# Reordering the write-out of the last two token groups: adds first, gates after both adds, a separate buffer for the last copy

## The chip, the cores and the metric

The kernel runs on one core of a Trainium2 chip. The metric is device time of one execution in microseconds (us).

Engines are called by the profile's short names: PE is TensorE, DVE is VectorE, ACT is ScalarE, POOL is GpSimd, SP is SyncE, which here issues the output transfers. A "q" behind a name (SPq) is that engine's sequencer.

## The reference, cut to what matters

```python
x = A_x                                  # (1, 2048, 1024) bf16
xn = _layernorm(x)
s = attention(xn, wqkv) @ wo             # 32 heads, window 8, dilation 2
g = silu(swiglu_mlp(xn, w1, w3, w2))     # hidden size 3584
return x + s * g                         # gate, then residual
```

Everything here takes place in the last stage: `@ wo` for the second half of the tokens, then `* g`, then `+ x`, then the transfer to memory.

## The kernel before

The large matrix products are done as seven half-size block products in place of eight (a Strassen-like scheme). For the output projection a group of 128-token tiles yields four blocks: 11, 12, 22 and 21 (first digit: half of the tokens, second: half of the columns). Blocks 11 and 21 come complete out of PE's accumulators and are copied by ACT. Blocks 12 and 22 need a saved PSUM tile added, by DVE. Each block is then multiplied by its gate and, in the second half of the tokens, gets its residual added (both DVE), and SP issues its transfer.

```python
def wo(b):
    ...
    for gp, ii in ((0, I), (1, I)) if b == 0 else ((0, I), (1, (0,)), (1, (1,))):
        ...                                    # the last group is cut in two for b == 1
        product(pa, gp, ii, a11, b11, True)    # tile "wa"
        product(pe, gp, ii, s1, t1, True)      # tile "we"
        flush()                                # the tail of the group before
        act_copy(pb, pa)                       # pb: tile "wb"
        act_copy(sp5, pe)                      # "wsp"
        ...
        product(pb, gp, ii, s2, t2, False)
        act_copy(su2, pb)                      # "wsu"
        steps = {
            "e12": lambda: (product(pe, gp, ii, s4, b22, False), finished(b, 0, 1, gp, ii, pe, su2)),
            "e22": lambda: (product(pb, gp, ii, s3, t3, False), finished(b, 1, 1, gp, ii, pb, sp5)),
            "e11": lambda: (product(pa, gp, ii, a12, b21, False), finished(b, 0, 0, gp, ii, pa)),
        }
        for k in ("e12", "e22", "e11") if n == 2 else ("e11", "e22", "e12"):
            steps[k]()

        def tail(gp=gp, ii=ii, pb=pb):         # block 21, in block 22's accumulator
            product(pb, gp, ii, a22, t4, False)
            finished(b, 1, 0, gp, ii, pb)
        ...

def finished(b, u, dh, gp, ii, ps, add=None):
    cut = slice(ii[0], ii[-1] + 1)
    g = g_tile(b, u, dh, gp)[:, cut]
    n = {(0, 0): 0, (1, 1): 2, (0, 1): 4, (1, 0): 0}[u, dh] + gp
    d = h_sb[:, 16 + 2 * n:18 + 2 * n, CH:][:, cut]
    rows_ = out_rows(out_flat, b, u, dh, gp)[:, cut]
    with hp():
        if add is None:
            nc.scalar.copy(out=d, in_=ps)                 # L956: blocks 11, 21
        else:
            nc.vector.tensor_add(d, ps, add)              # L958: blocks 12, 22
        anchor["v"] = nc.vector.tensor_mul(g, d, g)       # L959: gate
        if b == 0 or gp == 0:
            nc.gpsimd.dma_start(out=rows_, in_=g, accum_op=ALU.add)
        else:
            nc.vector.tensor_add(g, g, xw[u, dh][:, cut])  # L963: residual
            nc.sync.dma_start(out=rows_, in_=g)            # L964: transfer
```

A tile framework puts these instructions in order and adds the waits. Group names end in the order of the loop: the last two groups are `wa1_10` and `wa1_11` and so on; the profile leaves the numbers out. L151 is the matmul helper.

## Time and profile before

| | before |
|---|---|
| median of 3 runs | 723.38 us (723.37 to 723.46) |
| profiled execution | 723.18 us, span 721.5 us |
| last product of the last group begins on PE | 714.50 us |
| last DVE instruction ends | 717.39 us |
| last output transfer issued | 717.50 us |
| first matmul of this stage's first product | 690.99 us |

"Span" is what the trace covers; the time is 1.70 us more than it. The prediction shows the page, the chain and the timeline of the last microseconds. One view it names but doesn't show is that of the line that issues the output transfers, here for the time from 712 us on. Its columns are engine, operation, count, duration in ns as min/median/max, first and last start; the last line is the time from issue to landing of these five transfers.

```profile
L964 SPq DMA_DIRECT2D out_dram<-h_sb x5: 332/332/382, 712.7 to 717.5; - x5
...
DMA to landing us min/median/max: 1.7/1.7/3.0
```

Read it as: SP is occupied for 0.33 us by each issue; the data is in memory 1.7 us after the issue as a rule.

### The profile page before, as it was taken

What the parts mean: (1) busy time and instruction counts of PE and PEld (TensorE: products, weight loads), DVE (VectorE), ACT (ScalarE), POOL (GpSimd) and SP (SyncE); (2) the same over time, 40 slices, a digit from 0 to 9 for tenths busy, and PEclk for the clock granted to TensorE, in tenths of its full rate; (3) what the DMA queues carried; (4) which work ended last, traced back from release to release, by engine and by line L of the source; (5) the groups of instructions that cost most, each with busy time, mean ns of one, the idle gap of its engine ahead of it and who ended that gap; (6) DMA issues with size and microseconds to landing.
All of it is one profiled execution on the core that took longest, in us unless ns stands there. A gap on an engine that the chain in (4) does not pass through costs nothing.

```text
span 721.5 us, 8817 instructions
## 1 busy us (share of the span) xinstructions
PE 713.2 (99%) x3367; PEld 346.3 (48%) x3367; DVE 625.5 (87%) x697; ACT 314.0 (44%) x329; POOL 95.7 (13%) x162
## 2 busy tenths in 40 slices
PE   8999999999999999999999999999999999999996
PEld 6655565654444444444444444444444444444442
DVE  7996879779879878978999999969859989999964
ACT  5744334356555556545555312034364573020233
POOL 1011100012300000233111000000435005000011
PEclk9999999999999999999999999999999999999999
DMA  9956256787754523568756547469799444563615
GB/s 336 275 140 169 91 177 234 237 267 233 241 186 142 187 78 114 167 212 258 247 175 211 189 132 262 132 208 388 159 297 319 141 137 152 167 204 127 211 23 108
DMA packets 119242, 139.52 MB, mean 193 GB/s; under 512 B 17696, under 2 KB 94496, under 8 KB 118560
## 3 DMA queue, kind: packets, MB, share of 16 engines
q1 hardware_dynamic: 104656, 97.01, 42.7%
q0 software_dynamic: 14544, 41.95, 18.2%
q8 instruction: 26, 0.43, 0.2%
q14 instruction: 16, 0.13, 0.1%
HBM read 96.21 MB, written 38.80 MB: 187 GB/s over the span
## 4 chain that ended last, share of the span: by engine, by line
PE 95%; ACT 2%; DVE 2%; DMA 0%; issue 0%; DVEq 0%; ACTq 0%
PE bm L151 20%; PE am L151 13%; PE em L151 13%; PE db L151 10%; PE bq L151 9%; PE de L151 7%; PE da L151 7%; PE eq L151 6%; PE aq L151 3%; PE wb L151 2%; PE af L151 2%; PE wa L151 2%; PE we L151 2%; DVE h_sb L236 1%; PE af L1030 1%; DMA wring<-in_A_x_dram 0%
## 5 line engine op out<-in xcount | busy, mean ns | idle before, releaser
L151 PEld LDWEIGHTS <-wring 128*128 128x128 f16 (+1 forms) x1792 | 183.4, 102 | 204.3 <-issue 1.6
L151 PEld LDWEIGHTS <-h_sb 128*128 128x128 f16 (+1 forms) x1056 | 109.6, 104 | 118.1 <-issue 0.4
L151 PE MATMUL bm<-xs,wring 128*128 128x512 f16 x504 | 117.4, 379 | 0.1
L151 PE MATMUL am<-xT,wring 128*128 128x512 bf16 x336 | 79.7, 379 | 0.1
L151 PE MATMUL db<-wring,h_sb 128*128 128x512 f16 x336 | 73.2, 379 | 0.0
L481 DVE TENSOR_TENSOR BC<-Ep,vT 128x2048 bf16<-128x2048 bf16 x56 | 66.7, 1221 | 0.1
L426 DVE TENSOR_TENSOR pt<-qt,kT 128x4096 bf16<-128x4096 bf16 x24 | 55.0, 2292 | 0.6
L664 DVE TENSOR_TENSOR um<-em,um 128x1024 f32<-128x1024 f32 x28 | 34.2, 1223 | 21.0 <-PE em L151 20.2
L666 ACT ACTIVATE g<-um 128x1024 bf16<-128x1024 f32 x28 | 29.6, 1057 | 48.6 <-DVE um L664 48.6
L151 PE MATMUL da<-wring,h_sb 128*128 128x512 bf16 x224 | 49.0, 379 | 0.0
L467 POOL DMA_DIRECT2D Ep<-pb x64 | 38.0, 601 | 51.1 <-DVE pb L463 45.7
L151 PE MATMUL bm<-h_sb,wring 128*128 128x512 f16 x168 | 39.7, 379 | 0.0
L151 PE MATMUL em<-xT,wring 128*128 128x512 bf16 x168 | 39.7, 379 | 0.0
L151 PE MATMUL em<-xs,wring 128*128 128x512 f16 x168 | 39.7, 379 | 0.0
L491 DVE TENSOR_TENSOR oT<-oT,BC 128x2048 bf16<-128x2048 bf16 x32 | 39.1, 1221 | 0.3
L161 ACT COPY bm<-am 128x1024 f32<-128x1024 f32 x28 | 27.9, 998 | 25.8 <-PE am L151 25.8
L161 ACT COPY pm<-em 128x1024 f32<-128x1024 f32 x28 | 28.4, 1014 | 20.1 <-PE em L151 20.1
L161 ACT COPY um<-bm 128x1024 f32<-128x1024 f32 x28 | 28.4, 1014 | 18.9 <-PE bm L151 18.9
L685 ACT CAST g<-bm 128x1024 bf16<-128x1024 f32 x28 | 28.3, 1010 | 17.4 <-PE bm L151 17.4
L679 DVE TENSOR_TENSOR h_sb<-bm,pm 128x1024 bf16<-128x1024 f32 x21 | 25.6, 1219 | 5.1 <-PE bm L151 5.0
L428 DVE TENSOR_TENSOR pt<-pt 128x2048 bf16<-128x2048 bf16 x24 | 29.4, 1223 | 0.4
L489 DVE TENSOR_TENSOR BC<-BC 128x2048 bf16<-128x2048 bf16 x24 | 29.3, 1222 | 0.4
(191 smaller groups left out, 999.5 us busy)
## 6 DMA issues: line engine op xcount, KB each, us to landing
wring<-in_B_w_dram SPq DMA_DIRECT2D x61, 512.0 KB, 4.3
wring<-t_dram SPq DMA_DIRECT2D x16, 512.0 KB, 4.2
t_dram<-wring POOLq DMA_DIRECT2D x14, 512.0 KB, 3.9
wring<-t_dram SPq DMA_DIRECT2D x16, 384.0 KB, 5.0
wring<-in_B_w_dram SPq DMA_DIRECT2D x12, 384.0 KB, 4.5
wring<-in_A_x_dram SPq DMA_DIRECT2D x16, 256.0 KB, 4.8
Ep<-pb POOLq DMA_DIRECT2D x64, 64.0 KB, 4.7
wring<-in_A_wo_dram SPq DMA_DIRECT2D x8, 512.0 KB, 5.9
```

The costliest lines, as they stand in the source:

```text
L151: anchor["pe"] = nc.tensor.matmul(ps, lhsT=lhs[k], rhs=rhs[k], start=(first and k == 0), stop=(k == n - 1), skip_group_check=not first,)
L161: nc.scalar.copy(out=out_, in_=in_)
L426: nc.vector.tensor_mul(p_t[:], q[:], kT[:, :, o:o + CH])
L428: nc.vector.tensor_add(p_t[:, 0:4, :], p_t[:, 0:4, :], p_t[:, 4:8, :])
L467: nc.gpsimd.dma_start(out=pr[c][r:P:NR, :, sq * P:(sq + 1) * P], in_=pb[sq * 32:(sq + 1) * 32, :, :])
L481: nc.vector.tensor_mul(dst, E[:, w, :].unsqueeze(1).to_broadcast([P, n, CH]), vT[:, js, o:o + CH])
L489: nc.vector.tensor_add(B, B, C)
L491: nc.vector.tensor_add(A, A, B if w0 else C)
L664: v = nc.vector.tensor_add(su2[:], pe[:], su2[:])
L666: nc.scalar.activation(out=hl["g"][:, :, CH:], in_=su2[:], func=ACTF.Silu)
L679: anchor["v"] = nc.vector.tensor_add(h[:, :, CH:], pb[:], sp5[:])
L685: nc.scalar.copy(out=hl["g"][:, :, 0:CH], in_=pb[:])
```

## The change

The intent: DVE is overfull in the last microseconds. Blocks that need a PSUM add, the long kind of DVE instruction, should come early, while DVE still has idle time. Gate and residual of a block are put off until both adds are done. As block 11's gate now comes late, the last copy (block 21) may not reuse block 11's buffer and gets another one.

```diff
-            for k in ("e12", "e22", "e11") if n == 2 else ("e11", "e22", "e12"):
-                steps[k]()
+            rest = [steps[k]()[1] for k in ("e12", "e22", "e11")]
+            with behind("v2") if n == 1 else nullcontext():
+                rest[0]()
+            rest[1]()
+            rest[2]()
 
             def tail(gp=gp, ii=ii, pb=pb):
                 product(pb, gp, ii, a22, t4, False)
-                finished(b, 1, 0, gp, ii, pb)
+                finished(b, 1, 0, gp, ii, pb)()
...
-        n = {(0, 0): 0, (1, 1): 2, (0, 1): 4, (1, 0): 0}[u, dh] + gp
+        n = {(0, 0): 0, (1, 1): 2, (0, 1): 4, (1, 0): 4}[u, dh] + gp
...
             else:
-                nc.vector.tensor_add(d, ps, add)
-            anchor["v"] = nc.vector.tensor_mul(g, d, g)
-            ...
+                anchor["v2"] = nc.vector.tensor_add(d, ps, add)
+
+        def gate():
+            with hp():
+                anchor["v"] = nc.vector.tensor_mul(g, d, g)
+                ...                      # residual and transfer, as before
+        return gate
```

`behind("v2")` keeps the first gate behind the latest add in the order of issue.

## The prediction

> **What bounds the kernel now.** I read four views, from the whole to the place of the change. First the page: span, busy time and the summary of the chain that ended last.
>
> ```profile
> span 721.5 us, 8817 instructions
> ...
> PE 713.2 (99%) x3367; PEld 346.3 (48%) x3367; DVE 625.5 (87%) x697; ACT 314.0 (44%) x329; POOL 95.7 (13%) x162
> ...
> PE 95%; ACT 2%; DVE 2%; DMA 0%; issue 0%; DVEq 0%; ACTq 0%
> ```
>
> TensorE sets the time nearly everywhere: 95% of the chain is matmuls. A change that leaves the number of matmuls alone can win only where the chain is not on PE. The 2% for VectorE and 2% for ScalarE are the start and the end. The last stage is the output projection, done as seven block products. So I asked for the chain of work from 690 us on:
>
> ```profile
> 710.18 1.73 PE wb L151 x8
> 711.90 0.88 PE wa L151 x4
> 712.78 0.02 issue
> 712.80 0.59 ACT h_sb L956
> 713.40 0.02 issue
> 713.42 0.42 DVE h_sb L959
> 713.85 0.60 DVE h_sb L958
> 714.45 0.33 DVE h_sb L963
> 714.78 0.60 DVE h_sb L958
> 715.38 0.67 DVE h_sb L959 x2
> 716.05 0.34 DVE h_sb L963
> 716.38 0.34 DVE h_sb L959
> 716.72 0.33 DVE h_sb L963
> 717.05 0.34 DVEq L1264
> ```
>
> PE leaves the chain at 712.78 us, with the first product of the last group's output (block 11, tile wa) with three more products to come on PE. From 713.42 us on, DVE is the chain without a gap: L958 adds a PSUM tile to its saved copy (blocks 22 and 12), L959 multiplies by the gate, L963 adds the residual. The timeline of the same stretch gives the true starts:
>
> ```profile
> 711.75 0.42 DVE L959 TENSOR_TENSOR h_sb<-h_sb 128x512 bf16<-128x512 bf16 x1 [1.10 <-ACT h_sb L956]
> 712.21 0.42 DVE L963 TENSOR_TENSOR h_sb<-h_sb,xw 128x512 bf16<-128x512 bf16 x1
> 712.63 1.02 PE L151 MATMUL wb<-h_sb,oT 128*128 128x512 f16 x4
> 713.49 1.03 PE L151 MATMUL we<-wring,h_sb 128*128 128x512 bf16 x4
> 713.76 0.68 DVE L958 TENSOR_TENSOR h_sb<-wb,wsp 128x512 bf16<-128x512 f32 x1
> 714.50 1.02 PE L151 MATMUL wb<-wring,oT 128*128 128x512 f16 x4
> 715.60 0.59 ACT L956 CAST h_sb<-wb 128x512 bf16<-128x512 f32 x1 [2.22 <-PE wb L151]
> 716.63 0.76 DVE L963 TENSOR_TENSOR h_sb<-h_sb,xw 128x512 bf16<-128x512 bf16 x2
> ```
>
> The reader is to see three things. DVE idles from 712.63 to 713.42 while products finish, and is then overfull. The last product (block 21, wb at 714.50) comes late: four matmuls have a cadence of 0.86 us, so after 713.49 it could have begun at 714.35; it accumulates into the bank that block 22's add reads until 713.76 + 0.68 = 714.44. And its ScalarE copy ends at 715.60 + 0.59 = 716.19, while the last DVE instruction starts at 716.97 (716.63 + 0.76 - 0.42) and ends at 717.39: the end waits for DVE's queue, not for the last product. After that the last output transfer is issued at 717.50 and the median transfer of this line lands 1.7 us after issue; the rest up to 721.5 us is closing down, which the change doesn't touch.
>
> **What the Trainium skill says.** "VectorE: DVE Perf Modes", the perf-mode tier table: an add of two tensors runs at two elements per cycle with bf16 in SBUF, at one with a PSUM operand or fp32. The trace agrees: 0.68 us for an add from PSUM, 0.42 us for a bf16 one, of the same 512 columns. So a block that needs an add costs DVE more than one that is copied by ScalarE, and these are the blocks that the change puts first. The same page, "The DRAIN you can't avoid", says that the next operation waits for the pipe and that a semaphore adds nothing. [...]independent starts are 0.60 us apart behind an add and 0.34 behind a bf16 operation. It differs on the second: a residual add right behind the multiply it reads starts 712.21 - 711.75 = 0.46 us after it, 0.12 more. The measurement decides, and this 0.12 matters below. "Perfetto Trace Analysis", section "Optimizing Tensor Performance", wants independent matmul groups to rotate through PSUM banks so that emptying one overlaps the next; blocks 22 and 21 share a bank by construction, and the 0.15 us delay at 714.50 shows it.
>
> **The change part by part.** It removes and adds no arithmetic: the same matmuls, 20 DVE instructions, casts and transfers in the last two groups. I compared the instruction order of the two builds; outside the write-out they are alike.
>
> *The new PE order.* In each of the last two groups the products go 11, 22, 12, 21 before and 12, 22, 11, 21 after. Each is four matmuls, so slots stay at 711.74, 712.63, 713.49 and 714.50 in the last group. Block 12 needs ScalarE's copy of wb, which ends at 712.58, before its product ends at about 712.77; no new wait. Block 22's slot does not move, so its add cannot begin much before 713.76.
>
> *The new DVE order.* Block 12's add starts at about 712.77 + 0.11 = 712.88 (0.11 is the distance from a PE end to an idle DVE's start at 698.06 to 698.17), in time that was idle. It frees DVE at 713.48. Then block 22's add at 713.76, and the build has: multiply 12, multiply 22, residual 12, multiply 11, residual 22, residual 11, multiply 21, residual 21. Starts: 714.36, 714.70, 715.04, 715.37, 715.71, 716.04, 716.38; the last directly depends on the one before, so 716.38 + 0.46 = 716.84. End 716.84 + 0.42 = 717.26.
>
> *The sum.* Behind block 22's add, before had a residual add, a PSUM add and six more bf16 operations; after has eight bf16 operations. One PSUM add (0.60) leaves the chain, and block 11's multiply (0.34) comes into it, because its product is now third: 0.26 us less. But the old order ended with two independent residual adds (0.34 apart), the new one ends with a dependent pair (0.46): 0.12-0.13 us given back. Net 717.39 - 717.26 = 0.13 us.
>
> *A possible extra.* Before, block 22's add started exactly one 0.34 cadence behind block 11's multiply (713.42), so DVE may have held it. Its product's end is modelled at 713.65; ready could be 713.69 to 713.76 if the distance is 0.04 to 0.11. Up to 0.07 us more, and the last product moves by the same amount. I take 0.03.
>
> *The buffer.* Block 21's cast formerly reused block 11's buffer; now that block's gate comes late, it reuses block 12's, read by a multiply that ends near 714.78, well before the cast at 715.60. Without this the cast would wait for multiply 11 (to 715.79), some 0.2 us; with it, nothing. The buffer preserves the gain rather than makes one.
>
> *Elsewhere.* In the full-size groups the gating order shifts a little; in the first group at 508.59 us multiply 12 gets ahead of add 22, whose end moves from 509.81 to about 510.4, and PE needs that bank at 510.77. Tight, but hidden. The second-to-last group is covered by PE work: zero.
>
> **The rivals.** (a) *The last product becomes the bound*: its cast ends at 716.19, multiply 21 could start by 716.21 and the end be 717.09. DVE still binds by 0.17, so this caps the gain at 0.30 us if something on DVE is cheaper than I count: 723.1. (b) *Nothing*: if multiply 11 or add 22 is released later than I assume, the dependent pair eats everything: 723.4. The closeness of 0.26 and 0.12 speaks for it. (c) *Issue of outputs becomes the bound*: SyncE takes 0.34 us for each transfer, and the four outputs now come at least 0.33 us apart, the last 0.8 behind the third; it speaks against it. A collision would cost at most 0.1: 723.4. (d) *A stall in the middle*: if the 510.77 margin fails, up to 0.3 us lost: 723.6.
>
> **Range and chances.** 723.38 - 0.13 - 0.03 = 723.22 us, taken as 723.2. The argument covers 723.0 to 723.6. The profiled execution took 723.18 where the timed ones took 723.37 to 723.46, so another session may sit some tenths off; I take 722.7 to 723.8. A change of 2% would be 14.5 us, more than twice the 6 us that lie behind PE's last product at 715.52: faster 0.005, within 2% 0.99, slower 0.005.
>
> **What would show it.** Right: in the last group add 12 starts near 712.9, add 22 at 713.70 to 713.76, eight bf16 operations follow without a gap but one of 0.12 before the last, which ends near 717.2; PE's four slots unmoved, and the last still about 0.1 late. Wrong: add 22 later than 713.8, a gap before multiply 11 or 21, the last transfer's issue more than 0.15 behind the last add, PE's chain longer at 510 us, or the whole span moved while this stretch gained.

## The result, and the profile after

| | before | changed |
|---|---|---|
| median | 723.38 us (6 runs, 723.27 to 723.46) | 721.87 us (6 runs, 721.79 to 722.62) |
| ratio | | 0.9981 (95%: 0.9969 to 0.9994), within 2% |
| profiled execution | 723.18 us, span 721.5 | 721.83 us, span 720.1 |

A ratio here is the mean time of one kernel's fast runs over the mean of the other's of the same rounds, so it isn't quite the ratio of the medians. The gain is small, but it is 1.51 us by the medians and 1.35 us by the profiled executions where 0.16 us had been predicted, and the time lies below the predicted range.

First the page of the changed kernel: the same counts of arithmetic, and three instructions more in all than the 8817 before.

```profile
span 720.1 us, 8820 instructions
...
PE 712.5 (99%) x3367; PEld 346.2 (48%) x3367; DVE 625.6 (87%) x697; ACT 314.1 (44%) x329; POOL 95.7 (13%) x162
```

Then the end of the chain, from the stretch before PE leaves it. The columns are start, length, engine, tile and line; L961 is now the PSUM add, L965 the gate, L969 the residual.

```profile
713.05 0.90 PE wb L151 x4
713.95 0.02 issue
713.98 0.69 DVE h_sb L961
714.67 0.67 DVE h_sb L965 x2
715.33 0.34 DVE h_sb L969
715.67 0.33 DVE h_sb L965
716.00 0.67 DVE h_sb L969 x2
716.67 0.34 DVE h_sb L965
717.02 0.02 issue
717.04 0.42 DVE h_sb L969
```

As predicted, the chain enters DVE with block 22's add, eight bf16 instructions follow it without a gap but one ahead of the last. The timeline of the changed kernel gives the starts:

```profile
712.02 1.03 PE L151 MATMUL we<-wring,h_sb 128*128 128x512 bf16 x4
...
712.91 1.02 PE L151 MATMUL wb<-h_sb,oT 128*128 128x512 f16 x4
713.16 0.69 DVE L961 TENSOR_TENSOR h_sb<-we,wsu 128x512 bf16<-128x512 f32 x1 [0.30 <-PE we L151]
713.77 1.03 PE L151 MATMUL wa<-wring,oT 128*128 128x512 bf16 x4
713.98 0.69 DVE L961 TENSOR_TENSOR h_sb<-wb,wsp 128x512 bf16<-128x512 f32 x1
...
714.72 1.02 PE L151 MATMUL wb<-wring,oT 128*128 128x512 f16 x4
...
716.59 0.42 DVE L965 TENSOR_TENSOR h_sb<-h_sb 128x512 bf16<-128x512 bf16 x1
717.04 0.42 DVE L969 TENSOR_TENSOR h_sb<-h_sb,xw 128x512 bf16<-128x512 bf16 x1
```

The last DVE instruction ends at 717.46, which is *later* on the clock than the 717.39 of before. The reason is the start of the kernel: the first matmul of the first large product comes at 8.84 us, before at 8.56, and the first matmul of the last stage at 691.27 instead of 690.99. The whole middle is 0.28 us late and otherwise unmoved. So times of different kernels are compared from here on **relative to the stage's start**, the first matmul of this output projection. On that scale the last add ends at 26.19 us in the changed kernel and at 26.40 us before, 0.21 us earlier.

But the span is 1.35 us shorter. Where is the rest? It is behind the last DVE instruction. The same view of the issuing line as above, now of the changed kernel:

```profile
L970 SPq DMA_DIRECT2D out_dram<-h_sb x5: 332/332/382, 712.9 to 717.5; - x5
...
DMA to landing us min/median/max: 1.7/1.7/1.7
```

The longest landing went from 3.0 to 1.7 us, and in the records of the trace before, the 3.0 us are the last transfer's. The view of what SP waits for, first before and then changed (total us, times, longest), says the same: L1264 and L1272 are the end of the program.

```profile
SPq L1264 <- DMA out_dram<-h_sb: 2.2, 2, 1.7
```

```profile
SPq L1272 <- DMA out_dram<-h_sb: 0.9, 2, 0.6
```

A transfer is carried out in 16 parts, each with its own completion in the trace. Before, 15 parts of the last transfer had landed at 719.25 and the 16th landed at 720.50, 1.25 us later. In the changed kernel the 16th landed 0.03 us after the 15th. What was in that part's way is in the list of DMA queues for the time from 716 us on, first before, then changed (packets, MB, share of the 16 engines):

```profile
DMA packets 452, 0.41 MB, mean 59 GB/s; under 512 B 58, under 2 KB 451, under 8 KB 451
...
q1 hardware_dynamic: 451, 0.40, 16.9%
q14 instruction: 1, 0.01, 0.3%
```

```profile
DMA packets 576, 0.52 MB, mean 75 GB/s; under 512 B 64, under 2 KB 576, under 8 KB 576
...
q1 hardware_dynamic: 576, 0.52, 21.4%
```

Before, one packet of kind "instruction" falls into this time: 8 KB, at 719.06 us, for 0.31 us. In the records, nothing of the last transfer moves after it except eight 1 KB packets, one part's worth (128 KB in 16 parts), which start from 719.36 to 719.99, five of them taking 84 to 152 ns where such a packet otherwise takes 46. In the changed kernel, the packet of this kind came at 714.76, before the last transfer was issued. It is an engine fetching its next stretch of program. The Trainium skill, "Runtime: NRT & Kernel Launch", section "Instruction fetch mechanics", says that each engine's instruction memory is a queue refilled in blocks through a DMA queue driven by the sequencer, at a cost "mostly hidden". The trace agrees in that the packets of kind "instruction" have queues of their own (q14 here); that one fetch is not hidden would be new.

So the difference behind the stage's start adds up as follows (relative times; each row is the difference of two of the trace's records, taken before rounding):

| | before | changed | gain |
|---|---|---|---|
| end of the last DVE add | 26.40 | 26.19 | 0.21 |
| from there to the last issue | 0.11 | 0.03 | 0.09 |
| from the issue to the last part's landing | 3.00 | 1.67 | 1.33 |
| last part's landing + closing down = span's end | 29.51 + 0.97 = 30.48 | 27.89 + 0.96 = 28.85 | 1.63 |
| stage's start | 690.99 | 691.27 | -0.28 |
| span | 721.48 | 720.13 | 1.35 |

Only the closing down, 0.97 and 0.96 us, is what the change doesn't touch.

### The profile page after: what moved, and what is told of

Same layout as the page of the kernel before. It is cut to its first block, busy times and chain, and to the rows that moved or that the text cites. A ratio compares the mean times of both kernels' runs of the same rounds, so it can differ in the third digit from the quotient of the medians.

```text
span 720.1 us, 8820 instructions
## 1 busy us (share of the span) xinstructions
PE 712.5 (99%) x3367; PEld 346.2 (48%) x3367; DVE 625.6 (87%) x697; ACT 314.1 (44%) x329; POOL 95.7 (13%) x162
## 4 chain that ended last, share of the span: by engine, by line
PE 93%; DVE 2%; ACT 1%; DMA 1%; issue 1%; SPq 0%; DVEq 0%; ACTq 0%
PE bm L151 20%; PE am L151 13%; PE em L151 13%; PE bq L151 9%; PE db L151 8%; PE da L151 7%; PE de L151 6%; PE eq L151 6%; PE aq L151 3%; PE wb L151 3%; PE af L151 2%; PE wa L151 1%; PE we L151 1%; PE af L1038 1%; DMA wring<-in_A_wqkv_dram 1%
```

## The experiments

**Theories.** T1: the landing depends on the instruction fetch, and the change moved the fetch out of the way because it altered the number of instructions of one engine. The build's order shows two more waits on DVE (block 12's add now waits for PE and ACT together, in each of the two groups), and the trace has 836 DVE records where before has 834, and 506 instead of 505 for ACT. T2 (rival): the landing depends on how the last transfers follow one another on SP; before, the last two were issued 0.42 us apart, now 0.71. T3 (rival): the 3.0 us is chance and any rebuild would lose it.

All results, each kernel with 5 runs beside the kernel before on the same chip (9 runs); the first two rows are the 6 runs each of the result above. Columns in the middle come from the trace's records of the profiled run, in us relative to the stage's start. "Against drain" is the last issue minus the end of DVE's drain (the DRAIN record behind DVE's last instruction; it ends 0.05 us after the last add). "16th part" is the landing of the last part minus that of the 15th.

| kernel | median us | ratio (95%) | last add ends | last issue | against drain | issue to landing | 16th part | fetch at | end of span |
|---|---|---|---|---|---|---|---|---|---|
| before | 723.38 | 1 | 26.40 | 26.51 | +0.06 | 3.00 | 1.25 | 28.06 | 30.48 |
| changed | 721.87 | 0.9981 (0.9969-0.9994) | 26.19 | 26.22 | -0.02 | 1.67 | 0.03 | 23.49 | 28.85 |
| b_dve2 | 722.61 | 0.9989 (0.9975-1.0003) | 26.40 | 26.51 | +0.06 | 1.76 | 0.04 | 22.22 | 29.25 |
| b_act2 | 723.66 | 1.0006 (0.9993-1.0018) | 26.40 | 26.51 | +0.06 | 3.02 | 1.26 | 28.09 | 30.50 |
| a_dve_minus2 | 721.82 | 0.9978 (0.9966-0.9991) | 26.19 | 26.22 | -0.02 | 1.68 | 0.02 | 27.50 | 28.87 |
| b_dve1 | 722.77 | 0.9990 (0.9978-1.0003) | 26.40 | 26.51 | +0.07 | 1.75 | 0.02 | 22.25 | 29.23 |
| b_queue | 722.13 | 0.9983 (0.9970-0.9997) | 26.39 | 26.42 | -0.03 | 1.88 | 0.13 | 27.86 | 29.28 |
| a_minus2_late | 722.87 | 0.9995 (0.9982-1.0007) | 26.19 | 26.60 | +0.35 | 2.40 | 0.61 | 27.53 | 29.89 |
| a_late | 722.29 | 0.9985 (0.9973-0.9998) | 26.20 | 26.60 | +0.35 | 1.78 | 0.03 | 23.34 | 29.28 |
| a_no_buffer | 722.01 | 0.9982 (0.9969-0.9994) | 26.32 | 26.34 | -0.03 | 1.68 | 0.04 | 23.25 | 28.99 |
| a_again | 722.29 | 0.9983 (0.9971-0.9996) | 26.19 | 26.22 | -0.03 | 1.67 | 0.03 | 23.22 | 28.86 |
| order_only | 721.78 | 0.9976 (0.9962-0.9989) | 26.25 | 26.28 | -0.02 | 1.68 | 0.03 | 23.21 | 28.93 |
| order_buffer | 721.78 | 0.9976 (0.9963-0.9988) | 26.25 | 26.28 | -0.02 | 1.68 | 0.03 | 23.21 | 28.92 |
| a_pool | 723.78 | 1.0006 (0.9994-1.0019) | 27.48 | 27.50 | -0.02 | 1.69 | 0.02 | 23.16 | 30.16 |

The medians also hold the start: the stage began at 690.99 us in the profiled run of before and between 691.11 and 692.19 in the others. That scatter is larger than most differences between the parts of the change, so tenths are read from the last columns, not from the medians. All kernels gave correct results. The four runs from b_dve2 to b_dve1 in the table were made together, before the theory T4 below was formed; the next three to test it, and a_no_buffer with them; the last four to tell the parts of the change apart and to try a faster version.

### b_dve2 and b_act2: two idle instructions on DVE, or on ACT

Both are the kernel before with two small instructions more near the start of the program, far from anything critical; only the engine differs.

```diff
+    for i in range(2):
+        nc.vector.memset(const.tile([P, 1], FP32, name=f"fill{i}")[:], 0.0)      # b_dve2
```
```diff
+    for i in range(2):
+        nc.scalar.copy(out=const.tile([P, 1], FP32, name=f"fill{i}")[:], in_=scr[:])  # b_act2
```

> The kernel before with two tiny VectorE memsets (128x1) added at the start, where VectorE is idle. Theory F (fetch): the 8 KB instruction fetch that fell into the last output transfer at 719.06 us is VectorE's, due at a fixed place of its instruction stream; two more instructions put that place ahead of VectorE's final drain. Then the fetch moves to about 713.4 us, all 16 parts of the last transfer land within 1.7 us of issue instead of 3.0, and the time falls by 1.2 to 1.4 us, to 722.0 to 722.2, with the old order of blocks. Theory S (schedule): the gain came from the new order and the wider spacing of the last transfers; then this stays at 723.4.

> Control: the kernel before with two tiny ScalarE copies added at the start instead. Theory F with VectorE as the owner of the fetch: nothing moves, the fetch stays near 719.1 us and the time at 723.4 within 0.2. If ScalarE owned the fetch, the fetch would move and the time fall by over 1 us. Theory S: 723.4 as well.

The landing lines of these two, b_dve2 first:

```profile
L966 SPq DMA_DIRECT2D out_dram<-h_sb x5: 332/332/382, 713.3 to 718.1; - x5
...
DMA to landing us min/median/max: 1.7/1.7/2.0
```

```profile
L966 SPq DMA_DIRECT2D out_dram<-h_sb x6: 332/332/382, 712.0 to 718.7; - x6
...
DMA to landing us min/median/max: 1.7/1.7/3.0
```

With two idle instructions on DVE the fetch moves from 28.06 to 22.22 and the last landing falls from 3.00 to 1.76 us, with the schedule of the end exactly that of before (last add 26.40, last issue 26.51). (The 2.0 in the view is an earlier transfer.) With the same two on ACT, nothing moves at the end. The fetch is DVE's, T2 by itself and T3 fall for the kernel before, and T1 holds so far: 1.24 us can be had without changing which block comes first. It also gives what the schedule adds to that: with the fetch out of the way in both, b_dve2 ends at 29.25 and the changed kernel at 28.85, 0.39 us apart.

The medians show less. The five times of b_dve2 (722.22 to 722.79) all lie under the nine of before on its chip (723.23 to 723.52), but the interval of the ratio reaches 1, and the 722.0 to 722.2 expected was missed: in the profiled runs the stage of b_dve2 began 0.63 us later than that of before. For b_act2 it began 1.20 us later, and its median lies above the 723.4 within 0.2 that was expected.

### b_dve1: one idle instruction on DVE

```diff
+    for i in range(1):
+        nc.vector.memset(const.tile([P, 1], FP32, name=f"fill{i}")[:], 0.0)
```

> The kernel before with one tiny VectorE memset. Theory F: the fetch is due at the drain itself, which starts at 716.8 us, so it should come about 1.6 us later, near 718.4, and may hit the transfer before the last (issued at 717.08) or the last: a time between 722.0 and 723.5, the fetch time is the test. Theory S: 723.4.

The fetch came at 22.25, nearly where two instructions had put it, so my guess of its position was wrong. For the argument it says that one instruction is enough. This fits a kernel before that sits just at the edge of a block of its program, but no trace shows the block.

### a_dve_minus2: the changed kernel with two DVE instructions fewer

```diff
-    nc.vector.memset(eps_t[:], 1e-5)
+    nc.gpsimd.memset(eps_t[:], 1e-5)
...
-    untp(3, 1, dve_copy)
+    untp(3, 1, sc_copy)
```

Two DVE instructions near the start go to POOL and ACT, which brings the count back to 834.

> The changed kernel with two VectorE instructions taken away at the start: one 128x1 memset given to GpSimd, one PSUM copy of the first input block given to ScalarE. Theory F: the fetch falls again into the last transfer, near 719.1 us, its slowest part lands about 3.0 us after issue, and the time rises from 721.87 to 723.0 to 723.3. Theory S: 721.9, plus at most 0.3 for the copy that was moved.

This missed. The fetch did come back to the end (27.50), and the last landing stayed at 1.68 us:

```profile
DMA to landing us min/median/max: 1.7/1.7/1.7
```

So a late fetch is not enough to slow the transfer; T1 alone falls. What differs from before? The last transfer is issued at once: 0.03 us after the last add, 0.02 us *before* the end of DVE's drain, where before issued it 0.06 us behind it. In all of these traces the late fetch comes 1.25 to 1.64 us after the end of the drain. That suggested a theory T4: two things race for the same DMA part, the fetch that DVE sets off when it is through its last instruction, and the last output transfer; only if the transfer is issued second does one of its parts wait.

### b_queue: before, with block 12's transfer issued by another engine

T4 says that before would be cured without any change in the number of DVE instructions, if only its last transfer were issued before the drain ends. It comes late because SP is busy with the transfer ahead of it: that one was issued at 717.08 and occupies SP for 0.33 us, to 717.41, when the last add has ended at 717.39; with the wait between them, two issues in a row start 0.42 us apart (717.08 and 717.50). So this kernel gives block 12's transfer to ACT.

```diff
-                nc.sync.dma_start(out=rows_, in_=g)
+                (nc.scalar if (u, dh, ii[0]) == (0, 1, 1) else nc.sync).dma_start(out=rows_, in_=g)
```

> The kernel before, with the last but one output transfer (block 12 of the last group) issued from ScalarE's queue, so that SyncE is free for the last one: its issue should follow the last add by 0.03 us instead of 0.11, at about 717.42, just ahead of the end of VectorE's drain (717.44) instead of 0.06 behind it. VectorE's instruction count is unchanged. Theory R (race): the slow part of the last transfer comes only when that transfer is issued behind the end of the drain, which releases the fetch; then the fetch stays near 718.7 to 719.1 but the last transfer lands in 1.7 us, and the time falls to 722.0 to 722.2. Theory F without a race (any transfer of that moment is hit): 723.3.

It did what T4 says. The fetch stays late (27.86, and q14 is in the list for the last microseconds), the issue comes 0.03 us before the drain's end, and the landing takes 1.88 us instead of 3.00:

```profile
q1 hardware_dynamic: 424, 0.39, 15.8%
q10 hardware_dynamic: 144, 0.13, 5.5%
q14 instruction: 1, 0.01, 0.3%
...
DMA to landing us min/median/max: 1.7/1.7/1.9
```

The last line is from the view of the issuing line, L964. The time is 722.13 us. An issue that moved by 0.09 us earlier made the end 1.2 us earlier (30.48 to 29.28). But the edit does two things: it also takes a transfer off SP's queue, so that the issue ahead of the last one on this queue is 1.01 us away instead of 0.42.

### a_minus2_late and a_late: the reverse

T4 must also work backwards: the kernel a_dve_minus2 (late fetch, no harm), with a last issue that is delayed beyond the drain, must be slow again. An additional transfer of the same size to a scratch array is issued just ahead of the last one, on the same queue. a_late has the same additional transfer in the changed kernel itself, where the fetch is early; it measures what the additional transfer costs by itself.

```diff
                     nc.vector.tensor_add(g, g, xw[u, dh][:, cut])
+                    if (u, dh, ii[0]) == (1, 0, 1):
+                        nc.sync.dma_start(out=x_dram[:, 0, 0:1, :], in_=g)
                     nc.sync.dma_start(out=rows_, in_=g)
```

> The changed kernel with two VectorE instructions less (fetch behind the drain, which cost nothing in that run), and one more 128 KB transfer, to scratch memory, issued by SyncE just ahead of the last output: the last issue moves about 0.4 us behind the end of the drain. Theory R: now the race is lost, the slowest part of the last transfer lands about 3.0 us after issue, and the time is 721.82 + 0.4 + 1.2, about 723.4. Rival: the new schedule is immune, and only the later issue counts: 722.2 to 722.3.

> Control for the run before it: the changed kernel as it is (fetch at 714.8, long done) with the same additional transfer ahead of the last output. Theory R and its rival alike: only the later issue counts, 721.87 + 0.4 = 722.2 to 722.3, and all 16 parts land within 1.8 us.

What SP waits for at the end, in a_minus2_late and then in a_late:

```profile
SPq L1274 <- DMA out_dram<-h_sb: 1.1, 1, 1.1
```

```profile
SPq L1274 <- DMA out_dram<-h_sb: 0.4, 1, 0.4
```

The direction is as T4 says: both issue the last transfer 0.35 us behind the drain, and only the one with the late fetch has a late 16th part (0.61 us against 0.03) and a longer landing (2.40 against 1.78). In a_minus2_late itself, the additional transfer was issued 0.03 us before the drain's end and landed in 1.67 us. The size is not: I had expected the 1.25 us of before. Here the fetch was recorded only 0.93 us after the last issue, before 1.55 us after it, and in the records six packets of the transfer run behind all others (719.27 to 719.70), before eight. So the fetch seems to have caught the part when a quarter of it was done; this reading of the 0.61 us is an argument and no run settles it. The time of 722.87 us lies below the 723.4 expected for the same reason; a_late's 722.29 was as expected.

### a_no_buffer: the change without its buffer

```diff
-        n = {(0, 0): 0, (1, 1): 2, (0, 1): 4, (1, 0): 4}[u, dh] + gp
+        n = {(0, 0): 0, (1, 1): 2, (0, 1): 4, (1, 0): 0}[u, dh] + gp
```

> The changed kernel without its third part: the last copy uses block 11's buffer again. The prediction said that the cast of block 21 would then wait for block 11's multiply, some 0.2 us: the cast should start near 716.0 instead of 715.78, the last add end 0.1 to 0.2 later, and the time be 722.0 to 722.1; VectorE's count and so the fetch are as in the changed kernel. Rival: the multiply is not on the way, nothing moves, 721.9.

The last add ends at 26.32 instead of 26.19: the last copy waits until block 11's gate has read the buffer. The cast starts 0.31 us later (24.82 against 24.51 from the stage's start), of which 0.13 reach the end. So the buffer is worth 0.13 us, less than the 0.2 us of the prediction's estimate; the time, 722.01, was as expected.

### a_again, order_only, order_buffer: the parts, on one chip

a_again is the changed kernel, unaltered. order_only keeps only the new order of the products; order_buffer has the order and the buffer, but a gate follows its add at once as before.

```diff
-            rest = [steps[k]()[1] for k in ("e12", "e22", "e11")]
-            with behind("v2") if n == 1 else nullcontext():
-                rest[0]()
-            rest[1]()
-            rest[2]()
+            for k in ("e12", "e22", "e11"):
+                steps[k]()
...                                  # finished() as before; order_only also with the old buffer
```

> The changed kernel unchanged, as the reference of the other three runs of this call: 721.8 to 721.9 in most executions. Both theories alike.

> The kernel before with the new product order (12, 22, 11) in the last two groups alone: gates at once, old buffer. VectorE gets the two additional waits of the changed kernel, so by the fetch theory the fetch comes before the last transfer (near 714) and the slow part is gone: 722.0 to 722.3. Of this, the missing deferral lets the multiply of block 12 delay the add of block 22 and with it the last product by 0.2 to 0.3 us, and the old buffer costs 0.1. If the deferral or the buffer carried the gain: 723.0 or more.

> New product order and own buffer, gates at once: the deferral alone is missing. Fetch early as in the changed kernel. Block 12's multiply stands ahead of block 22's add, the last product starts 0.2 to 0.3 us later relative to the stage, the end 0.05 to 0.2 later than in the changed kernel: 721.9 to 722.1.

Relative to the stage's start the three end at 28.86, 28.93 and 28.92: the order of the products carries all of the gain but 0.06 us. It alone brings the two more waits on DVE (836 records in all three) and the free DVE time. Putting the gates behind both adds gains those 0.06 us (26.25 to 26.19), and the buffer nothing without it. The last product did start 0.24 us later without the deferral (23.69 against 23.45), as expected, but most of that did not reach the end, and both times (721.78) came out below what had been expected. By the medians the picture is reversed (722.29 against 721.78 twice), because in the profiled runs the stage of a_again began 0.45 and 0.63 us later than those of the other two; the changed kernel itself had it at 691.27 in one profiled run and at 691.74 in the other, so it is no property of the build alone, and what sets it is not known. I therefore take the three as equal.

### a_pool: an attempt at a faster version

Two of the last group's residual adds, of blocks 12 and 22, go to POOL to relieve DVE (with two idle DVE instructions to hold the fetch away).

```diff
-                    nc.vector.tensor_add(g, g, xw[u, dh][:, cut])
+                    eng = nc.gpsimd if ii[0] == 1 and u + dh != 0 and (u, dh) != (1, 0) else nc.vector
+                    eng.tensor_add(g, g, xw[u, dh][:, cut])
```

> An attempt at a better version: the changed kernel with the residual adds of blocks 12 and 22 of the last group on GpSimd, and two tiny VectorE memsets at the start so that VectorE's count, and the fetch, stay. If each GpSimd add takes under 0.7 us, VectorE's chain is shorter and the last multiply waits for ScalarE's copy only: the last add ends 0.2 us earlier, 721.65. If GpSimd takes over 1 us for each, SyncE, which issues in order, is held behind block 22's output and the end comes later: 722.2 or more.

It is 1.3 us slower than the changed kernel behind the stage's start (30.16 against 28.85). Its timeline:

```profile
714.94 2.08 DVE L967 TENSOR_TENSOR h_sb<-h_sb 128x512 bf16<-128x512 bf16 x3
...
715.59 2.44 POOL L972 TENSOR_TENSOR h_sb<-h_sb,xw 128x512 bf16<-128x512 bf16 x2 [6.74 <-DVE h_sb L967]
...
717.06 1.25 DVE L972 TENSOR_TENSOR h_sb<-h_sb,xw 128x512 bf16<-128x512 bf16 x1
```

POOL needs 1.22 us on average for each add that takes DVE 0.42 us (two in 2.44 us; spans on POOL are rough), and while it works DVE's own instructions stretch: a residual add takes 1.25 us instead of 0.42. The skill's "GPSIMD Engine Reference", section "Key points", says that POOL shares its interfaces to the on-chip memory with DVE and contends with DVE instructions that have two such inputs; this agrees with it. No version of these experiments clearly beats the changed kernel.

## Why the prediction was wrong

What it said of the schedule held nearly to the hundredth; what it left out, 1.33 us, was eight times the 0.16 us that it told of. In its own order (the changed kernel's times have 0.28 us taken off for the later start):

1. **PE's slots unmoved.** Predicted 711.74, 712.63, 713.49 and 714.50. Measured 711.74, 712.63, 713.49 and 714.44. Right; the last moved by 0.06 us because block 22's add came sooner, which the prediction had allowed for.
2. **Block 12's add in idle time, at 712.88.** Measured 712.88. Right.
3. **The sum of 0.13 us, with up to 0.07 more for block 22's add.** One PSUM add left the chain, one gate came in, and the dependent pair at the end stands 0.45 us apart (716.59 to 717.04) as against 0.34. Block 22's add came at 713.70, and of the possible 0.07 us there came 0.06, not the 0.03 taken. Measured: 0.21 us at the end of the last add. Right, with one term small by 0.03.
4. **The buffer.** The mechanism is right: without it the cast waits, by 0.31 us. Its worth at the end is 0.13 us and not 0.2.
5. **Elsewhere zero, with a tight place at 510 us.** Right: what shift there is (0.28 us) is there from 8.84 us on and stays the same past 510 us. "The whole span moved while this stretch gained" was one of the prediction's signs of being wrong; it did move, but later, so it hides 0.28 us of the gain and makes none.
6. **Rival (c), the issue of outputs.** It was asked of the changed kernel, where a collision was put at 0.1 us at most. The collision was in the kernel before, where SP was still issuing the previous transfer; its going away is 0.09 us by itself. If T4 is right, it is much more by way of the race.
7. **The step that failed.** "After that the last output transfer is issued at 717.50 and the median transfer of this line lands 1.7 us after issue; the rest up to 721.5 us is closing down, which the change doesn't touch." Both halves are wrong. The transfer that mattered was not a median one: it took 3.00 us, the maximum in the very same line of the view. And of the 4.1 us from the last DVE instruction to the span's end only 0.97 were closing down. With a landing of 1.7 us the span of before would have ended 1.3 us sooner, which could have been noticed: 717.50 + 1.7 + 0.97 is 720.2, not 721.5. The runs showed in its place a landing of 3.00 us before and 1.67 after, 1.33 us of the 1.63 gained behind the stage's start.

A second omission goes with it. "It removes and adds no arithmetic" is true, but the new order adds two waits on DVE, which are instructions too; they move the point at which DVE fetches the next stretch of its program. That the change also cured the late landing was luck: nothing in it aimed at that.

One reading of the skill's page on DVE in the prediction goes too far. Independent bf16 instructions start 0.34 us apart though each record is 0.42 us long, so one starts 0.08 us before the record in front has ended; the traces don't show that the next operation waits for the pipe to empty. Only the measured distances entered the sum, so nothing rests on it.

**What is shown of the cause.** The late landing needs a DVE fetch in the last microseconds: b_dve2 and b_dve1 take that away from the kernel before, and the late landing is gone. It needs a second thing as well, since a_dve_minus2 has the late fetch and lands in 1.68 us. T4 takes this to be a last issue behind the end of DVE's drain, and all five traces with a late fetch agree: before, b_act2 and a_minus2_late (at half the size) issue behind it and are slow, a_dve_minus2 and b_queue issue before it and are not. A rival fits these five as well: in the three slow ones the last issue also follows the one ahead of it on SP by 0.38 to 0.42 us, in the other two by 0.71 and 1.01. That closeness alone does no harm is shown (b_dve2 has 0.42 and lands in 1.76), but no run has a late fetch and tells the two apart. So it is shown that the second condition lies in how the last transfers are issued (b_queue changes nothing else); that the drain's end decides it is not shown.

What the reordering is worth depends on the fetch. With the fetch early in both (b_dve2 against changed) it is 0.39 us, of which 0.21 lie on DVE, 0.09 at the issue and 0.09 in the landing (1.76 to 1.67). With the fetch late in both (before against a_dve_minus2, 30.48 to 28.87) it is 1.62 us. The change takes both conditions away, so on this kernel the landing is cured twice.

The mechanism within the DMA is argued. The skill's "DMA: Bandwidth & Descriptors", section "Queues, rings and completion order", says that each DMA engine takes its queues in turn and finishes a whole packet of one before it turns to the next, and that row 14 belongs to the runtime, refills included. The trace agrees so far as it goes: the fetch is one 8 KB packet on q14 and exactly one of 16 parts is late. In the slow runs the packets of that part start behind the fetch's end (in before it ends 1.86 us after the issue, and the first of the eight starts at 1.86); in b_queue the last data packet has ended 0.05 us before the fetch starts, and in a_dve_minus2 no 1 KB packet starts after it. **What stays open:** why the fetch is recorded 1.25 to 1.64 us after the end of the drain; why the eight packets behind it took up to 152 ns each instead of 46, and why the whole delay is 1.25 us where the fetch itself took 0.31; why a_minus2_late shows half of it; and what sets the 0.1 to 1.2 us by which other builds start the stage later than before did.

## What to carry to other kernels

Account for the time behind the last compute instruction as you do for any other: take the last transfer's own landing, not the median, and check that issue, landing and closing down add up to the span. Where a rebuild moves the time by more than the schedule explains, try adding two idle instructions to one engine at a time in the old kernel: here it told a better schedule from a shifted instruction fetch. And compare short stretches from the start of their own stage, since the start of the program alone moved here by more than most parts of the change were worth.

## What the Trainium skill lacked or had wrong

- "Runtime: NRT & Kernel Launch", "Instruction fetch mechanics": it gives refill blocks of 16 KiB and calls the cost mostly hidden. The fetch that follows DVE's instruction count is here one packet of 8 KB on q14 (q8, the other queue of this kind, has packets of 16 KB), and it went with 1.25 us at the end of the kernel, because the last output transfer's 16th part landed that much behind the 15th. The page doesn't say that a fetch can hold up a data transfer.
- "VectorE: DVE Perf Modes", "The DRAIN you can't avoid": after a copy, a semaphore is said to add nothing. Here a residual add right behind the gate it reads starts 0.45 to 0.46 us after it, independent instructions 0.34 us apart.
- "GPSIMD Engine Reference", "Engine selection": an add of two inputs is put at about two times slower than on DVE. Here it was 1.22 us on average (POOL spans are rough) against 0.42, 2.9 times, and DVE's add beside it took 1.25 us.
- No page that I read says that an issue held up by the one ahead of it can change how long its transfer takes to land. SP's issues in a row start 0.42 us apart here; in before this put the last issue 0.11 us behind the add where b_queue has 0.03, and the landings were 3.00 and 1.88 us.
